# A delta rule on 32-row tiles and a soft mixture of experts: experts on the four column groups of TensorE, routing with phi as the stationary operand

## The chip, the cores and the metric

One core of a Trainium2 chip runs the whole program. The metric is the device time of one execution in microseconds (us); lower is better. Of three executions of the kernel before the median is 769.14 us (764.82 to 784.38). TensorE is called PE, VectorE DVE, ScalarE ACT, GpSimd POOL and SyncE SP, as the profile has them; SP issues most of the DMAs.

## The reference

```python
k_n = k / (norm(k) + 1e-6)                     # B=4, H=8, S=768, D=48
for t in range(S):                             # the delta rule
    y[t]  = q[t] @ state
    state = state + beta[t] * outer(k_n[t], v[t] - k_n[t] @ state)
x = y.transpose(0, 2, 1, 3).reshape(3072, 384)
logits = x @ phi                               # phi 384x32: 8 experts, 4 slots each
d = exp(logits - logits.max(0)); d /= d.sum(0) + 1e-9
slot_input = d.T @ x                           # 32x384
for e in range(8):                             # w1[e] 384x1024, w2[e] 1024x384
    slot_out[4e:4e+4] = relu(slot_input[4e:4e+4] @ w1[e]) @ w2[e]
c = softmax(logits, axis=1)
out = c @ slot_out                             # 3072x384
```

## The kernel before

Everything is float32. The sequence is cut into 24 chunks of 32 positions, four chunks to a group, so there are six groups (n = 0 to 5). A tile of 128 partitions holds 4 heads times 32 positions; the other two factors of 32 (batch, two head halves) lie in the free dimension. For each group the keys are normed (`norm`), transposed and multiplied into small 32x32 blocks (`prep`); the blocks go through DRAM (`ld`, then `lb`), a triangular inverse is worked out on DVE in 31 steps of two instructions (`invert`, tiles `pr` and `tt`, L248 and L251), and comes back through DRAM (`td`) as `TT`. `chunk` then runs the recurrence: `psR`/`psY` (state times keys and queries, L288), `psW` (L299), `psS` (new state, L309), `psY` (L326), with copies on DVE and ACT between them.

When a group is done its rows `Y` are routed (`route`): `logits(b)` transposes them (L346) and multiplies by `phi` (L352, the transposed rows stationary, 32 columns moving), `over_slots` and `maximum` make the two softmaxes with a running maximum, `sums` the running denominators, `repeat` copies `d` to four partition groups by a matmul with `sel` (L410), and `slots(c)` adds d.T @ x into `sacc`: POOL spreads `dr` with the mask `hm` to 128 columns (`db`, L420), and four matmuls with `Y` stationary follow (L425). The routing of group n-1 is handed out, merged with the inverse of group n+1, in chunks 2 and 3 of group n; a scheduler then orders every engine's instructions. Each engine works through its own list in order.

After the sixth group its routing is drained alone, the pools of the attention close, and a pool `wp2` opens on their memory. `first(e)` makes each expert's hidden row transposed (L524: w1 stationary, 4 slots moving, 32 matmuls an expert), `second(e)` multiplies by w2 (L535, 384 columns moving, all 32 slots stationary with zeros for the other experts). At the end `cT` (transposed c) times `so` gives 24 output tiles (L556), copied by ACT and DVE in turn (L561, L559) and stored. A float32 matmul shows as two instructions in the trace, a transpose as one. `load_w1` fills 96 partitions by two DMAs of 48 partitions each, `load_w2` 128 partitions; both go through SP's list. Two experts' w1 are loaded ahead, at the first chunk; the other 14 matrices (each 1536 KB) are loaded from `wp2`.

Of the kernel before, what the change touches and what calls it, by code (L numbers as in the profile page):

```python
# [16 lines left out]
def kernel(  # L17
# [21 lines left out]
    nc = tc.nc  # L39
# [13 lines left out]
    NFC = F // P  # L53
    assert G == 2 and B == 4 and GC * U == C and Dm == H * D and NSL == C
# [4 lines left out]
    ps = ctx.enter_context(tc.tile_pool(name="ps", bufs=1, space=PSUM))  # L59
    dp = ctx.enter_context(tc.tile_pool(name="dp", bufs=2, space=bass.MemoryType.DRAM))  # L60
    att = ExitStack()
    io = att.enter_context(tc.tile_pool(name="io", bufs=2))
# [65 lines left out]
    sel = cpool.tile([P, GC, 4, C], F32, name="sel")  # L128
    for h in range(4):
        nc.gpsimd.tensor_copy(sel[:, :, h, :], ident.rearrange("p (c t) -> p c t", t=C))  # L130
    ones = cpool.tile([P, 1], F32, name="ones")
    nc.vector.memset(ones, 1.0)
# [12 lines left out]

    def load_w1(e, pool, bufs):
        w1t[e] = pool.tile([GD, 4, F], F32, name="w1t", tag="w1t", bufs=bufs)
        for g in range(G):
            nc.sync.dma_start(
                out=w1t[e][g * D:(g + 1) * D],  # L150
                in_=moe_w1[e, g * 4 * D:(g + 1) * 4 * D].rearrange("(h d) f -> d h f", h=4))
# [126 lines left out]
    def chunk(cc, Yn, fill):  # L278
# [49 lines left out]
        nc.scalar.activation(Yn[:, c].rearrange("p b e -> p (b e)"),  # L328
                             py.rearrange("p b g d -> p (b g d)"), ACT.Copy)
# [3 lines left out]
    dsum = cpool.tile([P, NSL], F32, name="dsum")  # L333
    sacc = cpool.tile([GD, 4, NSL], F32, name="sacc")
    mrun = cpool.tile([NSL, 1], F32, name="mrun")
    mB = {}

    def route(n, Yn):
# [4 lines left out]
        def logits(b):  # L343
            py = pt([GD, GC, P])
            for c in range(GC):
                nc.tensor.transpose(py[:, c, :], Yn[:, c, b, :], ident)  # L346
            yT = wk.tile([GD, 4, GC, C], F32, name="yT", tag="yT")
            nc.scalar.activation(yT.rearrange("p h c t -> p c h t"),  # L348
                                 py.rearrange("p c (h t) -> p c h t", h=4), ACT.Copy)
            pl = pt([P, NSL])  # L350
            for h in range(4):
                nc.tensor.matmul(pl, lhsT=yT[:, h].rearrange("p c t -> p (c t)"),  # L352
                                 rhs=phi[:, h, :], start=(h == 0), stop=(h == 3))
            nc.vector.tensor_copy(lg[:, b, :], pl)
# [14 lines left out]
        def maximum():  # L369

            cm = small.tile([P, NSL], F32, name="cm", tag="cm")
            nc.vector.tensor_reduce(cm, lg.rearrange("p b s -> p s b"), axis=AX.X, op=ALU.max)
            pm = pt([NSL, P])
            nc.tensor.transpose(pm, cm, ident)
            if n == 0:
                nc.vector.tensor_reduce(mrun, pm, axis=AX.X, op=ALU.max)
            else:
                m1 = small.tile([NSL, 1], F32, name="m1", tag="m1")
                nc.vector.tensor_reduce(m1, pm, axis=AX.X, op=ALU.max)
                nc.vector.tensor_tensor(mrun, mrun, m1, op=ALU.max)  # L380
            pmb = pt([P, NSL])
            nc.tensor.matmul(pmb, lhsT=mrun.broadcast_to([NSL, P]), rhs=ident[0:NSL, 0:NSL],
                             start=True, stop=True)
            mB[n] = small.tile([P, NSL], F32, name="mB", tag="mB")
            nc.vector.tensor_copy(mB[n], pmb)
            nc.vector.tensor_tensor(d, lg, mB[n].unsqueeze(1).broadcast_to([P, B, NSL]),
                                    op=ALU.subtract)
            nc.scalar.activation(d, d, ACT.Exp)

        def sums():  # L390
            if n == 0:
                nc.vector.tensor_reduce(dsum, d.rearrange("p b s -> p s b"), axis=AX.X,
                                        op=ALU.add)
# [12 lines left out]
        def repeat():

            pd = pt([P, GC, B, NSL])
            for c in range(GC):
                nc.tensor.matmul(pd[:, c].rearrange("p b s -> p (b s)"),  # L410
                                 lhsT=sel[:, c].rearrange("p h t -> p (h t)"),
                                 rhs=d.rearrange("p b s -> p (b s)"), start=True, stop=True,
                                 skip_group_check=True)
# [3 lines left out]
        def slots(c):  # L417
            db = wk.tile([P, B, 4, NSL], F32, name="db", tag="db")
            for b in range(B):
                nc.gpsimd.tensor_tensor(  # L420
                    db[:, b], st["dr"][:, c, b].unsqueeze(1).broadcast_to([P, 4, NSL]),
                    hm.unsqueeze(2).broadcast_to([P, 4, NSL]), op=ALU.mult)
            pa = pt([GD, 4, NSL])
            for b in range(B):
                nc.tensor.matmul(pa.rearrange("p h s -> p (h s)"), lhsT=Yn[:, c, b, :],  # L425
                                 rhs=db[:, b].rearrange("p h s -> p (h s)"),
                                 start=(b == 0), stop=(b == B - 1))
            if n == 0 and c == 0:
                nc.vector.tensor_copy(sacc, pa)
            else:  # L430
                nc.vector.tensor_tensor(sacc, sacc, pa, op=ALU.add)

        return ([lambda b=b: logits(b) for b in range(B)] + [over_slots, maximum, sums, repeat]
# [32 lines left out]
    for e in range(NW1):  # L466
        load_w1(e, wpool, NW1)
    routing = []
    for n in range(NG):
        Yn = wk.tile([P, GC, B, GD], F32, name="Y", tag="Y")  # L470
# [29 lines left out]
    wp2 = ctx.enter_context(tc.tile_pool(name="wts2", bufs=1))  # L500
    for e in range(E):
        if e >= NW1:
            load_w1(e, wp2, 4)
        load_w2(e, wp2, 5)
    pd = pt([NSL, 1])
    nc.tensor.matmul(pd, lhsT=dsum, rhs=ones, start=True, stop=True)
    rd = cpool.tile([NSL, 1], F32, name="rd")
    nc.vector.tensor_scalar(rd, pd, 1e-9, None, op0=ALU.add)
    nc.vector.reciprocal(rd, rd)

    hx = wp2.tile([P, E, NFC, NSL], F32, name="hx")
    nc.gpsimd.memset(hx, 0.0)
    pso = ps.tile([NSL, Dm], F32, name="pso", tag="psRW")

    def first(e):

        sl = slice(e * SPE, (e + 1) * SPE)
        st = {}

        def product(t):  # L520
# [70 lines left out]
```

## Time and profile before

| | us |
|---|---|
| median of three executions | 769.14 |
| lowest and highest | 764.82, 784.38 |
| profiled execution: time | 777.74 |
| its span, first to last instruction | 776.0 |
| PE matmul busy in it | 507.6 |
| DVE, ACT, POOL busy | 255.6, 112.6, 109.6 |
| mean granted clock of TensorE | 0.655 of 2.4 GHz |

The profile is of one execution, 8.6 us above the median. Its span is divided in three: up to 566 us the six groups, 566 to 597 us the last routing, 597 to 776 us experts and output. The busy share of PE is high in the last part and middling in the first, where DVE, PE, POOL and DMA follow one another.

### The profile page before, as it was taken

What the parts mean: (1) busy time and instruction counts of PE and PEld (TensorE: products, weight loads), DVE (VectorE), ACT (ScalarE), POOL (GpSimd) and SP (SyncE); (2) the same over time, 40 slices, a digit from 0 to 9 for tenths busy, and PEclk for the clock granted to TensorE, in tenths of its full rate; (3) what the DMA queues carried; (4) which work ended last, traced back from release to release, by engine and by line L of the source; (5) the groups of instructions that cost most, each with busy time, mean ns of one, the idle gap of its engine ahead of it and who ended that gap; (6) DMA issues with size and microseconds to landing.
All of it is one profiled execution on the core that took longest, in us unless ns stands there. A gap on an engine that the chain in (4) does not pass through costs nothing.

```text
span 776.0 us, 20231 instructions
## 1 busy us (share of the span) xinstructions
PE 507.6 (65%) x9068; PEld 393.3 (51%) x9068; DVE 255.6 (33%) x694; ACT 112.6 (15%) x222; POOL 109.6 (14%) x158
## 2 busy tenths in 40 slices
PE   0603617128880488508892298863868999999998
PEld 0502516116770377406671177652757957767643
DVE  2139302781228522492237712563211000000012
ACT  0301201003220133102221022210212000000011
POOL 4121100220050300502041200422004000000000
PEclk9955557556665576755965557855767576666665
DMA  6250395404520135103540022001103999910023
GB/s 115 41 116 7 67 173 85 86 6 89 109 38 1 46 66 109 19 0 67 86 85 2 32 37 62 3 1 41 17 2 126 241 251 243 230 48 1 1 100 144
DMA packets 147639, 58.10 MB, mean 75 GB/s; under 512 B 131680, under 2 KB 142944, under 8 KB 147552
## 3 DMA queue, kind: packets, MB, share of 16 engines
q1 hardware_dynamic: 141888, 55.87, 33.1%
q10 hardware_dynamic: 5664, 0.94, 0.7%
q8 instruction: 71, 1.16, 0.6%
q14 instruction: 16, 0.13, 0.1%
HBM read 45.76 MB, written 11.01 MB: 73 GB/s over the span
## 4 chain that ended last, share of the span: by engine, by line
PE 59%; DVE 19%; DMA 7%; ACT 4%; POOL 4%; issue 3%; SPq 2%; ACTq 0%
PE ph L524 11%; PE pso L535 7%; DVE tt L251 7%; DVE pr L248 7%; PE pt L199 5%; PE pt L352 5%; PE pt L425 4%; PE psW L299 4%; PE psR L288 4%; PE pout L556 4%; PE pt L214 3%; PE psY L326 3%; DMA TT<-td 2%; PE psS L309 2%; PE pt L346 2%
## 5 line engine op out<-in xcount | busy, mean ns | idle before, releaser
L199 PE MATMUL pt<-ident,Ks 128*128 128x128 f32 x96 | 39.9, 418 | 172.1 <-POOL Ks L183 137.7
L199 PEld LDWEIGHTS pt<-ident,Ks 128*128 128x128 f32 x96 | 19.9, 207 | 177.4 <-POOL Ks L183 163.3
L524 PEld LDWEIGHTS ph<-sacc,w1t 96*128 96x128 f32 x512 | 88.2, 274 | 4.2 <-issue 3.8
L524 PE MATMUL ph<-sacc,w1t 96*128 96x4 f32 x512 | 88.8, 312 | 0.2 <-ACT cT L545 0.2
L248 DVE TENSOR_TENSOR pr<-tt,lb 128x31 f32<-128x31 f32 (+15 forms) x186 | 75.9, 408 | 20.1 <-POOL lb L236 15.0
L251 DVE TENSOR_TENSOR tt<-tt,pr 128x31 f32<-128x31 f32 (+15 forms) x186 | 68.3, 367 | 5.3
L299 PE MATMUL psW<-R,TT 32*32 32x48 f32 x1536 | 37.2, 233 | 35.4 <-DMA TT<-td 32.9
L535 PE MATMUL pso<-w2t,hx 128*32 128x384 f32 x128 | 56.9, 613 | 1.7 <-DVE hx L528 1.7
L299 PEld LDWEIGHTS psW<-R,TT 32*32 32x32 f32 x1536 | 28.4, 127 | 45.7 <-issue 23.5
L528 DVE TENSOR_SCALAR hx<-ph 128x32 f32<-128x32 f32 x8 | 1.5, 192 | 141.1 <-PE ph L524 141.1
L214 PE MATMUL pt<-KQ 48*32 48x64 f32 x1536 | 41.0, 284 | 6.9 <-issue 5.0
L352 PE MATMUL pt<-phi,yT 96*128 96x32 f32 x192 | 36.9, 346 | 8.7 <-ACT yT L348 8.6
L425 PE MATMUL pt<-db,Y 128*96 128x128 f32 x192 | 35.4, 356 | 8.3 <-POOL db L420 8.3
L352 PEld LDWEIGHTS pt<-phi,yT 96*128 96x128 f32 x192 | 34.1, 266 | 13.1 <-ACT yT L348 12.0
L202 ACT ACTIVATE KQ<-pt 128x512 f32<-128x512 f32 x48 | 28.5, 597 | 76.9 <-PE pt L199 76.9
L288 PE MATMUL psR<-S,KQ 128*32 128x96 f32 x768 | 34.2, 313 | 7.7 <-DVE S L319 6.0
L302 DVE COPY U<-psW 128x384 f32<-128x384 f32 x24 | 13.4, 558 | 77.6 <-PE psW L299 77.6
L199 PE MATMUL pt<-ident,Qs 128*128 128x128 f32 x96 | 38.3, 403 | 0.0
L214 PEld LDWEIGHTS pt<-KQ 48*32 48x32 f32 x1536 | 28.4, 138 | 18.8 <-ACT KQ L202 10.1
L420 POOL TENSOR_TENSOR db<-dr,hm 128x128 f32<-128x128 f32 x96 | 35.7, 411 | 13.6 <-ACT dr L415 13.6
L425 PEld LDWEIGHTS pt<-db,Y 128*96 128x96 f32 x192 | 31.8, 223 | 11.5 <-POOL db L420 10.2
L321 ACT ACTIVATE S<-psS 48x768 f32<-48x768 f32 x23 | 18.5, 804 | 127.7 <-PE psS L309 127.7
(103 smaller groups left out, 577.3 us busy)
## 6 DMA issues: line engine op xcount, KB each, us to landing
w1t<-in_moe_w_dram SPq DMA_DIRECT2D x16, 768.0 KB
w2t<-in_moe_w_dram SPq DMA_DIRECT2D x8, 1536.0 KB
Ks<-in_k_dram SPq DMA_DIRECT2D x96, 48.0 KB
V<-in_v_dram SPq DMA_DIRECT2D x96, 48.0 KB
out_dram<-ob SPq DMA_DIRECT2D x24, 192.0 KB
Qs<-in_q_dram SPq DMA_DIRECT2D x80, 48.0 KB
ld<-Lc SPq DMA_DIRECT2D x24, 128.0 KB
lb<-ld SPq DMA_DIRECT2D x6, 512.0 KB
```

The source lines that it names most:

```text
L199: nc.tensor.transpose(tp[:, i, a, :], src[:, c, b * G:(b + 1) * G, :].rearrange("p g d -> p (g d)"), ident)
L214: nc.tensor.matmul(pg[g][rh, b], lhsT=KQ[cc][r, b, 0, rh], rhs=KQ[cc][r, b, :, rh], start=True, stop=True, skip_group_check=True)
L248: nc.vector.tensor_tensor(prv, tt[:, 0:m, j:j + 1].broadcast_to([P, m, w]), lb[:, j, j + 1:C].unsqueeze(1).broadcast_to([P, m, w]), op=ALU ...
L251: nc.vector.tensor_tensor(tt[:, 0:m, j + 1:C], tt[:, 0:m, j + 1:C], prv, op=ALU.subtract)
L288: nc.tensor.matmul(dst[hs[h], b].rearrange("p g d -> p (g d)"), lhsT=kq[:, b, a, hs[h]], rhs=old[:, h, b, :], start=(b == 0), stop=False, ...
L299: nc.tensor.matmul(pw[hs[h], u], lhsT=T[hs[h], u], rhs=R[hs[h], u], start=(u == 0), stop=True, skip_group_check=True)
L352: nc.tensor.matmul(pl, lhsT=yT[:, h].rearrange("p c t -> p (c t)"), rhs=phi[:, h, :], start=(h == 0), stop=(h == 3))
L420: nc.gpsimd.tensor_tensor(db[:, b], st["dr"][:, c, b].unsqueeze(1).broadcast_to([P, 4, NSL]), hm.unsqueeze(2).broadcast_to([P, 4, NSL]), o ...
L425: nc.tensor.matmul(pa.rearrange("p h s -> p (h s)"), lhsT=Yn[:, c, b, :], rhs=db[:, b].rearrange("p h s -> p (h s)"), start=(b == 0), stop ...
L524: nc.tensor.matmul(st["ph"][:, t, :], lhsT=w1t[e][:, h, t * P:(t + 1) * P], rhs=sacc[:, h, sl], start=(h == 0), stop=(h == 3))
L535: nc.tensor.matmul(pso, lhsT=hx[:, e, t, :], rhs=w2t[e][:, t, :], start=(e == 0 and t == 0), stop=(e == E - 1 and t == NFC - 1))
L556: nc.tensor.matmul(po, lhsT=cT[:, n, b, :], rhs=so, start=True, stop=True)
```

## The change

The routing, the expert stage and the output are written with stationary operands of 32 columns or 32 rows, so that four matmuls stand on four different 32-column groups (or 32-row groups) of the array. The delta rule itself (`norm`, `prep`, `invert`, `chunk`) stays, save that `Y` gets four more columns of ones behind its 96 and is one of two fixed tiles.

- Routing: `turn(b)` only transposes; one `logits` for the whole group multiplies with `phi` stationary (32 columns), one batch to each column group, and transposes the result back. `maximum` keeps its running maximum repeated on four partition groups and works out one factor `al` per slot. `sums` is gone: the column of ones makes the denominator in `sacc`. `repeat` takes 32 columns of the identity instead of `sel`; `slots` has 16 matmuls a chunk with 32 rows, 32 columns and 97 moving, on the four diagonal tiles, and nothing on POOL.
- Experts: four experts at a time, each on its own column group; the slots are stationary and w1 moves (512 columns), `hr` is masked, transposed by 8 transposes, and w2 moves (384 columns). At the end one matmul with `sel4` adds the four groups.
- Output: the four batches' `cT` lie on four row groups, the tiles go through six PSUM banks and six `ob` buffers instead of four and four.
- Weights: w1 and w2 lie with 12 KB in one piece per partition on 128 partitions. `wp2` and the new PSUM pool `pp` wait tile by tile for the memory they take over (`reuse_waits="tile"`), and the loads are issued in another order.

```diff
+        w1t[e] = pool.tile([P, NKT, F], F32, name="w1t", tag="w1t", bufs=bufs)
+        nc.sync.dma_start(out=w1t[e], in_=moe_w1[e].rearrange("(p k) f -> p k f", k=NKT))
-        nc.sync.dma_start(out=w2t[e], in_=moe_w2[e].rearrange("(t p) d -> p t d", p=P))
+        nc.sync.dma_start(out=w2t[e], in_=moe_w2[e].rearrange("(p t) d -> p t d", t=NFC))
...
+        def logits():
+            pl = pt([P, P])
+            for h in range(4):
+                for b in range(B):
+                    nc.tensor.matmul(pl[C * b:C * b + C], lhsT=phi[:, h, :],
+                                     rhs=st["yT"][:, b, h].rearrange("p c t -> p (c t)"),
+                                     start=(h == 0), stop=(h == 3), skip_group_check=True)
+            lT = wk.tile([P, P], F32, name="lT", tag="lT", bufs=1)
+            nc.scalar.activation(lT, pl, ACT.Copy)
+            pq = pt([P, P])
+            nc.tensor.transpose(pq, lT, ident)
+            nc.vector.tensor_copy(lg.rearrange("p b s -> p (b s)"), pq)
...
+                nc.vector.tensor_tensor(m1, mrun, m1, op=ALU.max)
+                nc.vector.tensor_tensor(al, mrun, m1, op=ALU.subtract)
+                nc.scalar.activation(al, al, ACT.Exp)
+                nc.vector.tensor_copy(mrun, m1)
...
         def slots(c):
-            db = wk.tile([P, B, 4, NSL], F32, name="db", tag="db")
+            pa = pt([P, GD + 1])
             for b in range(B):
-                nc.gpsimd.tensor_tensor(
-                    db[:, b], st["dr"][:, c, b].unsqueeze(1).broadcast_to([P, 4, NSL]),
-                    hm.unsqueeze(2).broadcast_to([P, 4, NSL]), op=ALU.mult)
...
+                for h in range(4):
+                    r = slice(C * h, C * h + C)
+                    nc.tensor.matmul(pa[r], lhsT=st["dr"][r, c, b, :], rhs=Yn[r, c, b, 0:GD + 1],
+                                     start=(b == 0), stop=(b == B - 1), skip_group_check=True)
...
+    wp2 = ctx.enter_context(tc.tile_pool(name="wts2", bufs=1, reuse_waits="tile"))
+    for e in range(E):
+        if e >= NW1:
+            load_w1(e, wp2, 4)
+        if e % 4 == 3:
+            for i in range(e - 3, e + 1):
+                load_w2(i, wp2, 6)
...
+    def first(q):
...
+        def product(f):
+            ph = bank("ph", [P, HF])
+            for k in range(NKT):
+                for j in range(4):
+                    nc.tensor.matmul(ph[C * j:C * j + C], lhsT=sl[:, k, :],
+                                     rhs=w1t[4 * q + j][:, k, f * HF:(f + 1) * HF],
+                                     start=(k == 0), stop=(k == NKT - 1), skip_group_check=True)
...
+    def second(q):
+        for t in range(NFC):
+            for j in range(4):
+                nc.tensor.matmul(pso[C * j:C * j + C], lhsT=hT[q][:, t, C * j:C * j + C],
+                                 rhs=w2t[4 * q + j][:, t, :],
+                                 start=(q == 0 and t == 0), stop=(q == 1 and t == NFC - 1),
+                                 skip_group_check=True)
...
+    first(0)
+    second(0)
+    first(1)
+    second(1)
...
+            po = bank(("ph", "tr", "po")[i % 3], [P, Dm])
+            nc.tensor.matmul(po, lhsT=cT[C * b:C * b + C, n, :], rhs=so[C * b:C * b + C],
+                             start=True, stop=True)
+            ob = wp2.tile([P, Dm], F32, name="ob", tag="ob", bufs=6)
```

PE's list in group 3, from the last product with `phi` to the slots, before (`x4` is four matmuls of one kind in a row; the size is that of the output):

```order
L352 MATMUL pt<-phi,yT 128x32 x4
L326 MATMUL psY<-U,AT 32x48 x8
L288 MATMUL psR<-S_182,KQ 32x96 x9
L374 MATMUL pt<-ident,cm 32x128
L288 MATMUL psR<-S_182,KQ 32x96 x7
L288 MATMUL psY<-S_182,KQ 32x96 x13
L382 MATMUL pt<-ident,mrun 128x32
L288 MATMUL psY<-S_182,KQ 32x96 x3
L410 MATMUL pt<-d,sel 128x128 x4
L425 MATMUL pt<-db,Y 96x128 x15
L299 MATMUL psW<-R,TT_178 32x48
```

The same place after (L349 are the logits, L355 the transpose back, L402 the repeat, L414 the slots):

```order
L340 MATMUL pt<-ident,Y_581 96x128 x4
L320 MATMUL psY<-U,AT 32x48 x32
L349 MATMUL pt<-yT,phi 32x128 x16
L282 MATMUL psR<-S_175,KQ 32x96 x5
L355 MATMUL pt<-ident,lT 128x128
L282 MATMUL psR<-S_175,KQ 32x96 x11
L282 MATMUL psY<-S_175,KQ 32x96 x16
L379 MATMUL pt<-ident,cm 128x128
L391 MATMUL pt<-ident,mrun 128x32
L402 MATMUL pt<-d,ident 32x128 x16
L414 MATMUL pt<-Y_581,dr 32x97 x34
```

The four products of L352, spread among the chunk's matmuls, became one run of 16 behind the transposes; the order from there to the slots stays.

POOL's list in group 3, before (`lb` is the scaling that the inverse starts from, L236):

```order
L366 TENSOR_TENSOR Call<-el,mx 128x128
L420 TENSOR_TENSOR db<-dr,hm 128x128 x16
L236 TENSOR_TENSOR lb<-lb,bb 128x1024
L169 TENSOR_TENSOR sq<-Ks_80 128x1536
L183 TENSOR_TENSOR Ks_80<-Ks_80,rn 128x32x48
```

The same place after:

```order
L368 TENSOR_TENSOR Call<-el,mx 128x128
L230 TENSOR_TENSOR lb<-lb,bb 128x1024
L163 TENSOR_TENSOR sq<-Ks_80 128x1536
L177 TENSOR_TENSOR Ks_80<-Ks_80,rn 128x32x48
L249 TENSOR_TENSOR tt<-tt,bb 128x1024
```

The spreading of `dr` is gone, and `lb` stands right behind `Call`; so it does in group 4.

SP's list at the end of the groups, before, with what each row waits for:

```order
L268 DMA TT_178<-td 32x8x32 [waits DMAHW1_49,PE_49]
L155 DMA w2t<-in_moe_w_dram 128x8x384 [waits DMAHW3_49,DMAHW2_49,DMAHW4_49,DMAHW1_49,DMAHW5_49,DMAHW0_49,DMAHW6_49,DVE_49,DMAHW7_49,PE_49,Activation_49]
L155 DMA w2t<-in_moe_w_dram 128x8x384
L149 DMA w1t<-in_moe_w_dram 48x4x1024 x2
L155 DMA w2t<-in_moe_w_dram 128x8x384
```

After (L145 loads w1, L149 loads w2):

```order
L262 DMA TT_171<-td 32x8x32 [waits DMAHW7_49,PE_49]
L145 DMA w1t<-in_moe_w_dram 128x3072 [waits DMAHW0_49]
L145 DMA w1t<-in_moe_w_dram 128x3072 [waits DMAHW3_49,DMAHW4_49,DMAHW2_49,DMAHW5_49,DMAHW1_49,DMAHW6_49,DVE_49,DMAHW7_49,PE_49,Activation_49]
L149 DMA w2t<-in_moe_w_dram 128x3072 [waits Activation_49]
...
L145 DMA w1t<-in_moe_w_dram 128x3072 [waits DMAHW0_49,PE_49]
L145 DMA w1t<-in_moe_w_dram 128x3072 [waits DMAHW1_49,PE_49]
L149 DMA w2t<-in_moe_w_dram 128x3072 [waits DMAHW2_49]
```

The first load no longer waits for an engine. In the program as built the PE wait of the second load is for `psW` of the last chunk, and the PE waits below the gap (w1 of experts 6 and 7, the ninth and tenth load) are for the products of `first(0)` that read their buffers last.

## Rows read from the trace of the kernel before

**Rows 1.** Busy time by stage: us, busy us (count) by engine, clock, DMA share, GB/s

```profile
97.00:116.00 19.00, 3.00 (x67) 2.77 (x67) 1.37 (x4) 0.48 (x1) 0.00 (x0) 0.59 1.01 177
116.00:566.00 450.00, 274.49 (x7367) 226.27 (x7369) 201.09 (x547) 83.36 (x158) 78.98 (x109) 0.65 0.24 47
...
597.00:744.00 147.00, 145.09 (x642) 104.81 (x640) 1.54 (x8) 0.79 (x2) 0.00 (x0) 0.67 0.61 146
```

**Rows 2.** The chain that ended last, in order of time: start, us, what

```profile
347.66 2.82 POOL Ks L183
...
437.95 2.82 POOL Ks L183
...
491.17 5.41 POOL db L420 x15
496.58 1.87 POOL lb L236
...
532.61 2.35 POOL tt L255
...
744.96 27.65 PE pout L556 x48
```

**Rows 3.** PE, POOL and DVE in group 3 in order of time: start, us, instruction

```profile
379.12 0.84 PE L288 MATMUL psY<-S,KQ 128*32 128x96 f32 x32
...
389.06 1.09 PE L346 MATMUL pt<-ident,Y 128*96 128x128 f32 x4
...
391.19 1.92 PE L352 MATMUL pt<-phi,yT 96*128 96x32 f32 x8
...
400.53 5.47 PE L425 MATMUL pt<-db,Y 128*96 128x128 f32 x30 [1.23 <-POOL db L420]
...
400.07 5.77 POOL L420 TENSOR_TENSOR db<-dr,hm 128x128 f32<-128x128 f32 x16 [0.85 <-ACT dr L415]
...
413.12 0.55 DVE L293 TENSOR_TENSOR R<-V,psR 128x384 f32<-128x384 f32 x1 [2.33 <-PE psR L288]
```

**Rows 4.** PE in order of time: matmuls on four column groups (L288) and diagonal tiles (L299)

```profile
378.44 0.87 PE L288 MATMUL psR<-S,KQ 128*32 128x96 f32 x32
...
546.41 1.51 PE L288 MATMUL psR<-S,KQ 128*32 128x96 f32 x32
...
549.12 1.50 PE L299 MATMUL psW<-R,TT 32*32 32x48 f32 x64
...
562.91 0.88 PE L299 MATMUL psW<-R,TT 32*32 32x48 f32 x64
```

**Rows 5.** Busy time by short stretches, columns as in rows 1

```profile
378.00:380.00 2.00, 1.92 (x90) 1.69 (x91) 1.04 (x3) 0.45 (x2) 0.00 (x0) 1.00 0.46 73
546.00:551.00 5.00, 4.60 (x129) 3.92 (x129) 0.78 (x2) 0.00 (x0) 0.00 (x0) 0.55 0.01 3
...
596.00:600.00 4.00, 3.72 (x32) 3.25 (x32) 0.00 (x0) 1.57 (x4) 0.00 (x0) 1.00 1.05 388
...
680.00:684.00 4.00, 3.71 (x12) 2.23 (x13) 0.19 (x1) 0.00 (x0) 0.00 (x0) 0.50 0.52 119
...
748.00:752.00 4.00, 4.00 (x9) 2.05 (x8) 0.95 (x2) 0.98 (x2) 0.00 (x0) 0.56 0.68 245
```

**Rows 6.** Groups by line and shape: count, busy us, mean ns, idle before

```profile
L535 PE MATMUL pso<-w2t,hx 128*32 128x384 f32 x128 | 56.9, 613 | 1.7 <-DVE hx L528 1.7
```

**Rows 7.** PE in the last routing in order of time

```profile
566.84 0.32 PE L346 MATMUL pt<-ident,Y 128*96 128x128 f32 x1 [0.60 <-ACT Y L328]
...
578.39 1.92 PE L352 MATMUL pt<-phi,yT 96*128 96x32 f32 x8 [0.74 <-ACT yT L348]
...
587.17 5.83 PE L425 MATMUL pt<-db,Y 128*96 128x128 f32 x32 [1.23 <-POOL db L420]
```

**Rows 8.** SP's waits (us, times, longest) and SP in order of time

```profile
SPq L155 <- PE pt L425: 28.6, 1, 28.6
...
593.07 1.03 SPq L155 DMA_DIRECT2D w2t<-in_moe_w_dram  x2
```

More of the change, by code (lines that the diff above doesn't have):

```diff
@@ L53 @@
     NFC = F // P
+    NKT = Dm // P
     assert G == 2 and B == 4 and GC * U == C and Dm == H * D and NSL == C
@@ L127 @@
     nc.vector.tensor_reduce(tri, bdm.rearrange("p h t -> p t h"), axis=AX.X, op=ALU.add)
[L128 to L132, printed above, removed]
     TTs = [wk.tile([P, U, C], F32, name=f"TT{i}", bufs=1) for i in range(2)]
@@ L467 @@
         load_w1(e, wpool, NW1)
+    Ys = [wk.tile([P, GC, B, GD + 4], F32, name=f"Y{i}", bufs=1) for i in range(2)]
+    for t in Ys:
+        nc.gpsimd.memset(t[:, :, :, GD:GD + 4], 1.0)
     routing = []
     for n in range(NG):
-        Yn = wk.tile([P, GC, B, GD], F32, name="Y", tag="Y")
+        Yn = Ys[n % 2]
         more = n + 1 < NG
@@ L503 @@
             load_w1(e, wp2, 4)
[L504 to L508, printed above, removed]
-    nc.vector.reciprocal(rd, rd)
[L511 to L520, printed above, removed]
-            if t == 0:
-                st["ph"] = ps.tile([P, NFC, SPE], F32, name="ph", tag="pt", bufs=2)
-            for h in range(4):
-                nc.tensor.matmul(st["ph"][:, t, :], lhsT=w1t[e][:, h, t * P:(t + 1) * P],
-                                 rhs=sacc[:, h, sl], start=(h == 0), stop=(h == 3))
-        def relu():
-            nc.vector.tensor_scalar(hx[:, e, :, sl], st["ph"], 0.0, None, op0=ALU.max)
-        return [lambda t=t: product(t) for t in range(NFC)] + [relu]
@@ L532, in second, with bank @@
-    def second(e):
-        def product(t):
-            nc.tensor.matmul(pso, lhsT=hx[:, e, t, :], rhs=w2t[e][:, t, :],
-                             start=(e == 0 and t == 0), stop=(e == E - 1 and t == NFC - 1))
-        return [lambda t=t: product(t) for t in range(NFC)]
-    cT = wp2.tile([NSL, NG, B, P], F32, name="cT")
+        if e % 4 == 3:
+            for i in range(e - 3, e + 1):
+                load_w2(i, wp2, 6)
+    def bank(tag, shape):
+        return pp.tile(shape, F32, name=tag, tag=tag, bufs=2)
@@ new lines @@
+    sel4 = wp2.tile([P, 4, C], F32, name="sel4")
+    nc.vector.tensor_reduce(sel4[:, 0, :], ident.rearrange("p (c t) -> p t c", t=C), axis=AX.X,
+                            op=ALU.add)
+    nc.vector.tensor_copy(sel4[:, 1:4, :], sel4[:, 0, :].unsqueeze(1).broadcast_to([P, 3, C]))
+    rd = cpool.tile([P, 1], F32, name="rd")
+    nc.vector.tensor_scalar(rd, sacc[:, GD:GD + 1], 1e-9, None, op0=ALU.add)
+    nc.vector.reciprocal(rd, rd)
+    pT = bank("tr", [NSL, 4, G, D])
+    for h in range(4):
+        nc.tensor.matmul(pT[:, h].rearrange("p g d -> p (g d)"), lhsT=ident[:, C * h:C * h + C],
+                         rhs=sacc[:, 0:GD], start=True, stop=True, skip_group_check=True)
@@ L541 @@
+    def second(q):
[4 more added lines that the diff above has]
+                                 start=(q == 0 and t == 0), stop=(q == 1 and t == NFC - 1),
+                                 skip_group_check=True)
+    cT = wp2.tile([P, NG, P], F32, name="cT")
     for n in range(NG):
-        pc = pt([NSL, B, P])
-        for b in range(B):
-            nc.tensor.transpose(pc[:, b, :], Call[:, n, b, :], ident)
+        pc = bank("tr", [P, P])
+        nc.tensor.transpose(pc, Call[:, n].rearrange("p b s -> p (b s)"), ident)
@@ L545 @@
         nc.scalar.activation(cT[:, n], pc, ACT.Copy)
-    for e in range(E + 1):
-        drain(merge(*([second(e - 1)] if e else []), *([first(e)] if e < E else [])))
-    so = cpool.tile([NSL, Dm], F32, name="so")
-    nc.vector.tensor_scalar(so, pso, rd, None, op0=ALU.mult)
-    pp2 = ctx.enter_context(tc.tile_pool(name="pp2", bufs=1, space=PSUM))
+    first(0)
+    second(0)
+    first(1)
+    second(1)
+    sj = wp2.tile([P, Dm], F32, name="sj")
+    nc.vector.tensor_copy(sj, pso)
+    ps4 = bank("ph", [P, Dm])
@@ L552 @@
+    nc.tensor.matmul(ps4, lhsT=sel4.rearrange("p b t -> p (b t)"), rhs=sj, start=True, stop=True)
+    so = wp2.tile([P, Dm], F32, name="so")
+    nc.vector.tensor_scalar(so, ps4, rd, None, op0=ALU.mult)
     for n in range(NG):
```

123 lines of the change are left out of this document (63 added, 60 removed).

## The prediction

> **What bounds the kernel now.** I read the busy time by stage first [rows 1]. From 597 to 744 us PE is busy 145 of 147 us and nothing else is but the DMAs, at 61% of their time. Before 566 us PE is busy 61% of the time and DVE 45%, and no engine fills the stage: there the chain of waits tells more [rows 2]. Its last piece is PE's output product, 27.65 us, so the last 179 us are PE's. In it a group is a cycle of some 89 to 90 us (the scaling of the keys on POOL at 347.66 and again at 437.95). One stretch lies outside the cycle: from 97 to 116 us PE is busy 3 of 19 us [rows 1]. Third, the lists of PE, POOL and DVE in group 3 in order of time [rows 3]: PE runs the chunk's matmuls mixed with the routing from 380 us, the last product with `phi` ends at 393.1, the slots begin at 400.5 behind the first `db`, and the inverse stands on DVE behind `R` of the next group's first chunk (L293, 413.1 to 413.7). From there to 437.9, when POOL scales the keys, DVE works through the inverse and PE has nothing. So PE's time in the routing of groups 1 to 3 counts in full, and DVE's inverse is a term that the change doesn't touch. In group 4 the inverse begins later, at 498.5, behind POOL's `lb`, which stands behind 15 `db` [rows 2].
>
> **What the tiles are worth.** All prices of the new matmuls come from two of the old ones that already stand on four column groups or four diagonal tiles [rows 4]. `psR` is 16 matmuls of 96 columns on four column groups (x32 instructions): 0.87 us in a stretch with the clock granted at 2.4 GHz and 1.51 in one that lies almost all at 1.2 (mean 0.55 of full, [rows 5]). `psW` is 32 matmuls of 48 columns on four diagonal 32x32 tiles: 0.88 and 1.50 us. Both make 0.57 ns a column at the faster level, while the second expert product, one matmul at a time, takes 56.9 us for 64 matmuls of 384 columns, 2.3 ns a column [rows 6]. So four tiles side by side cost about what one costs, and I scale by columns.
>
> [...]
>
> **The change part by part**, against the span of 776.0 us.
>
> *a. w1 loaded ahead (97 to 116 us).* The `TT` load waits behind two experts' w1, 3.15 MB, which came at 177 GB/s with the DMA engines fully busy [rows 1], so for 17 us. These go to 48 partitions each. The w2 loads, to 128 partitions, came at 388 GB/s at the start of the expert stage [rows 5]. After, w1 goes to 128 partitions as well: 3.15 MB at 388 is 8.1 us. PE and SP both wait there, so what follows moves along: -8 us, bounds 0 and -9.5.
>
> *b. Routing in groups 1 to 3.* PE's list stays in order, so I add up what stands between the end of `psY` (380.0) and the first inverse step. To the end of the logits: 16 transposes (1.09 us for four at the slower clock, [rows 3], so 0.6 to 1.09), `psW` 0.9 to 1.5, `psS` and `psY` about the same each, and the logits, 16 matmuls of 128 columns, 1.2 to 2.0 by `psR`. Sum 6.4 to 10.9, taken 7.5 since the stretch starts at the faster level: 387.5 instead of 393.1. From there to the slots 7.4 us now; added are a copy on ACT and a transpose, a copy of `cm` and three tiny DVE instructions, some 1.4 us by like ones, and 0.4 for the repeat (1.2 to 2.0 for the 1.16 it is now). Slots begin at 396.7. They are 64 matmuls of 97 columns, 4.04 times `psW`: 3.6 to 6.1 us, taken 4.8, for the 5.9 us now, which POOL's 16 `db` pace (5.77 us, [rows 3]). Together -5 us a group, bounds -1 and -8; three groups -15. The inverse starts earlier by the same. `lb`, which followed the `db`, now follows `Call` and is out of the way; what could be late next is the load it scales, for which POOL doesn't wait now.
>
> *c. Group 4.* With the `db` gone, `lb` is no longer last; the DVE list then starts the inverse behind the second of four slot sums. By b, a cycle of 90 us later, the slots begin at 487 and their half is done at 489.5: -9. The stretch to the last inverse step, 34.1 us with the routing of group 4 inside against 24.2 in group 3, holds DVE's waits for PE's routing; part of these go: -3. Sum -12, bounds -5 and -15.
>
> *d. The last routing.* Now 566.8 to some 597 [rows 7]: four times transpose, copy, product, to 580.3, slots 587.2 to 593.0, then `cT`. After: the transposes follow each other, paced by PE at about 1.1 us, to 571; logits 2.0; the same 6.9 us and 1.4 more; slots 3.6 to 6.1, taken 5.5, to 587. Then `sacc` is turned (4 matmuls, 3 transposes, two copies, 3 us) and three `cT` go ahead in PE's list, 1 us. The experts start at 591.
>
> *e. Experts.* PE has 48 matmuls of 512 and 64 of 384 columns. By `psR` each half of either takes 7.0 to 12.1 us, 28 to 48 in all, for 145 now. So the loads decide: 14 matrices of 1.573 MB, 4.05 us each at 388 GB/s. Now the first of them waits 28.6 us for the last slots [rows 8] and goes out at 593.1. After, one goes out behind the last `TT` and the next seven when `psW` of the last chunk is done, at 563.8 in today's time [rows 4]; all eight are in by 594. Expert 6's w1 then needs a buffer that `first(0)` (591 to 600, at 9 us) gives back: six loads from 600, 24.3 us, and 2 us to land: 626.5. PE meanwhile does 8 transposes (4 us), `second(0)` (9), `first(1)` (9) and 8 more transposes (4), which ends at 626 also. `second(1)` needs the last matrix: 9 us, 635.5; copy, `sel4` product, scaling: 638. Now 744.9. If PE stays at 1.2 GHz throughout it is 650, at 2.4 and 388 GB/s 634.
>
> [...]
>
> *f. Output.* Stores carry 4.72 MB. In the one window where they weren't starved they moved 245 GB/s at 68% of the DMA engines [rows 5], so 360 at full: 13.1 us, with 1 us to the first copy and 2.5 for the last to land 17 us. PE's row groups would have to overlap for that, as in `psW`; if they don't it stays at 31 (27.65 us of PE, [rows 2]). Taken 17, nearest to `psW`, which also has 32 rows: 655.
>
> Sum: -8 -15 -12 -121 = -156. Span 620, and with the 1.7 us around it 622 for the profiled execution of 777.7. That one lies 8.6 us over the median; by the ratio 0.799 the median of 769.1 becomes 614; rounded with an eye to the bounds of b and e, which have more room below, 612.
>
> **Rivals.** (1) *The loads come no faster than now.* All 22 MB took from 593 to some 682 [rows 5, 8], 247 GB/s, 6.4 us a matrix. If 128 partitions aren't what made w2 fast (the window of 388 is the stage's first full one), the eighth is in at 611 and the last at 650: +24, 636. For it: w2's later windows mix with w1 and tell nothing. Against: w1 alone made 177 at 97 us, which with 388 for w2 gives the mean.
>
> (2) *The shorter routing is swallowed before the inverse,* by DVE's list or a lower clock: b and c give nothing, 639. Against: the chain goes through PE's slots in every group.
>
> (3) *Row tiles take turns in one bank.* One at a time a matmul of 128 columns takes 0.36 us (16 in 5.83, [rows 7]); 64 of 97 columns would take 17.7 us, 13 more in each of four groups and in the last routing: 612 + 65 = 677.
>
> (4) *The loads don't start early,* because one wait in the long list of the second load is the routing's after all: loads from 587, the eighth in at 615, +15: 627. That would be the change not doing what its pool says.
>
> (5) *Slower: neither row nor column groups overlap.* The logits, repeat and slots cost 5.8, 5.8 and 17.7 us, 17 us a group more than now and 22 more in the last routing than forecast; the expert products take 0.89 us each by columns, 114 us, so they end at 716 and the output at 747: 747 + 22 + 66 - 8 = 827, some 820 by the ratio. It beats the old time from the point where four tiles side by side take as long as about three in turn; `psR` and `psW` say one.
>
> **How the numbers follow.** The forecast, 0.72 (own range 590 to 632: e between 634 and 650, b and c by their bounds, f up to 14 us worse); (1) 0.11, (2) 0.06, (4) 0.05, (3) 0.02, (5) 0.02; 0.02 lies with mishaps that leave it within 2%, about what a measurement of this kernel can tell from no change. The range takes in (1), (2) and (4) and on the low side loads and clock at their best: 588 to 646. Faster 0.96, same 0.02, slower 0.02.
>
> **What would show it.** Right: w1 at over 350 GB/s near 97 us and the `TT` wait halved; groups of about 84 us; slots of 4 to 6 us with no POOL in them; loads busy from 30 us before the experts; the two expert products at some 7 to 12 us a half, with a wait for the last w2; output near 17 us. Wrong: loads below 300 GB/s, expert matmuls at over 1 ns a column, groups still at 89 us, output matmuls one after another.

## The result and the profile after

The changed kernel takes 610.31 us (median of four, 607.18 to 612.48); the kernel before took 776.26 (median of four in the same comparison, 764.82 to 784.38). The ratio is 0.794, 95% interval 0.788 to 0.800; it is taken over fast executions alone, and two of the four before (784.38 and 783.39) were slow, so it lies above the quotient of the two medians, 0.786. The profiled execution took 610.76 us with a span of 609.0; the span before was 776.0.

Busy time near the first wait, of the kernel after: stretch, us, busy us (count) of PE, its weight loads, DVE, ACT and POOL, granted clock, DMA share, GB/s.

```profile
100.00:104.00 4.00, 2.24 (x64) 2.00 (x64) 1.28 (x4) 0.40 (x1) 0.00 (x0) 0.80 0.92 336
104.00:108.00 4.00, 0.00 (x0) 0.00 (x0) 0.00 (x0) 0.00 (x0) 0.00 (x0) 0.63 0.98 403
```

The two w1 that came at 177 GB/s [rows 1] now come at about 400. The chain of the same execution (start, us, what) shows the `TT` load behind them and then the groups:

```profile
89.04 2.80 DMA td<-tt
...
100.27 10.51 DMA TT<-td
110.92 1.92 PE psW L293 x64
...
161.59 2.75 POOL Ks L177
...
210.02 2.87 PE pt L414 x128
...
244.18 2.79 POOL Ks L177
...
328.37 2.79 POOL Ks L177
...
377.98 3.13 PE pt L414 x72
381.17 1.46 PE pt L414 x52
...
412.78 2.79 POOL Ks L177
...
481.43 5.44 PE pt L414 x128
...
491.42 2.35 POOL tt L249
```

The same places in the chain of the kernel before, as far as the rows above lack them:

```profile
86.14 2.82 DMA td<-tt
...
115.86 2.02 PE psW L299 x64
...
166.36 2.75 POOL Ks L183
...
222.29 5.83 PE pt L425 x32
...
258.62 2.82 POOL Ks L183
...
597.37 23.54 PE ph L524 x128
```

L177 is the scaling of the keys, L414 the slots. Where the scalings stood 90.3 us apart (347.66 and 437.95, [rows 2]) they now stand 84.4 apart, and the `tt` of group 4 comes 78.6 us after the last of them (before 94.7). No `db` of POOL is left in the chain, and group 3's slots, at 378.0, take some 4.6 us. The last routing in the chain:

```profile
527.10 0.33 PE pt L340
...
528.10 1.82 PE pt L340 x8
...
530.59 1.60 PE pt L349 x26
...
539.57 5.44 PE pt L414 x128
...
548.38 0.98 PE ph L553 x2
```

From the first transpose (527.10) to the first expert product it is 21.3 us; before it was from 566.84 [rows 7] to 597.37, 30.5 us. Then the expert stage, first by stretches (columns as above), then by line (busy us, mean ns of one, idle before), then in the chain:

```profile
528.00:552.00 24.00, 18.48 (x239) 12.47 (x243) 5.08 (x24) 4.96 (x15) 0.83 (x4) 0.72 1.01 424
552.00:556.00 4.00, 4.00 (x34) 1.20 (x26) 0.00 (x0) 0.69 (x1) 0.00 (x0) 1.00 0.18 74
...
560.00:580.00 20.00, 13.89 (x114) 4.59 (x106) 1.44 (x2) 1.27 (x2) 0.00 (x0) 0.99 1.00 423
580.00:584.00 4.00, 1.75 (x12) 0.60 (x16) 0.00 (x0) 0.00 (x0) 0.00 (x0) 0.50 0.07 28
...
596.00:600.00 4.00, 4.00 (x15) 3.24 (x16) 2.06 (x4) 1.89 (x4) 0.00 (x0) 0.57 1.03 366
```

```profile
L553 PE MATMUL ph<-w1t,sl 128*32 128x512 f32 x96 | 14.7, 597 | 1.8 <-DMA w1t<-in_moe_w_dram 1.8
L577 PE MATMUL pso<-w2t,hT 128*32 128x384 f32 x128 | 14.4, 558 | 5.9 <-DMA w2t<-in_moe_w_dram 5.4 <-ACT hT L567 0.6
```

```profile
564.45 17.76 DMA w2t<-in_moe_w_dram
582.25 7.36 PE pso L577 x58
...
591.87 0.58 PE ph L603
```

The loads run at 424 GB/s from 20 us ahead of the first product. One of the eight went out at 512; at the next SP's list stood 11.2 us, so from 520 to 524 the DMAs moved 6 GB/s. The reader is to see two things more: the hole at 552 to 556, where SP's list stands at the first w1 that needs a buffer back, and that the last w2, not PE, starts the last half of the second product. After that load 58 of the half's 64 instructions take 7.36 us, where all 64 of the first half took 5.4: the granted clock was 0.50 at 580 to 584, at whose start PE still waited for that load. Mean ns are not costs here: 597 ns an instruction times 96 would be 57 us, the busy time is 14.7, so four run at once. The output begins at 591.9 and ends with the span at 609.0, 17.1 us.

### The profile page after: what moved, and what is told of

It reads as the page before. It is cut to its first block, busy times and chain, and to the rows that moved or that the text cites. A ratio compares the mean times of both kernels' runs of the same rounds, so it can differ in the third digit from the quotient of the medians.

```text
span 609.0 us, 20685 instructions
## 1 busy us (share of the span) xinstructions
PE 333.6 (55%) x9387; PEld 252.6 (41%) x9387; DVE 253.1 (42%) x661; ACT 113.5 (19%) x232; POOL 71.2 (12%) x62
## 4 chain that ended last, share of the span: by engine, by line
PE 44%; DVE 26%; DMA 12%; issue 5%; ACT 5%; SPq 4%; POOL 3%; ACTq 0%; DVEq 0%
DVE pr L242 9%; DVE tt L245 9%; PE pt L193 7%; PE psW L293 5%; PE pt L208 4%; PE pt L414 4%; PE psR L282 4%; PE psY L320 3%; PE psS L303 3%; DMA w2t<-in_moe_w_dram 3%; PE psY L282 3%; PE pt L340 3%; PE pso L577 2%; DMA TT<-td 2%; DMA Qs<-in_q_dram 2%
## 5 line engine op out<-in xcount | busy, mean ns | idle before, releaser
L313 DVE COPY S<-psS 48x768 f32<-48x768 f32 x23 | 22.1, 960 | 46.0 <-ACT S L315 46.0
L282 PE MATMUL psR<-S,KQ 128*32 128x96 f32 x768 | 31.8, 303 | 8.5 <-DVE S L313 6.0
L213 DVE TENSOR_TENSOR AT<-pt,tri 128x128 f32<-128x128 f32 x48 | 12.0, 286 | 58.6 <-ACT Lc L212 58.6
L320 PE MATMUL psY<-U,AT 32*32 32x48 f32 x1536 | 29.4, 233 | 4.9 <-issue 4.1
L177 POOL TENSOR_TENSOR Ks<-Ks,rn 128x1536 f32<-128x1536 f32 x6 | 16.6, 2770 | 123.7 <-DVE pr L242 88.8
L282 PE MATMUL psY<-S,KQ 128*32 128x96 f32 x768 | 29.9, 297 | 1.7 <-issue 1.7
L282 PEld LDWEIGHTS psR<-S,KQ 128*32 128x32 f32 x768 | 23.4, 135 | 14.4 <-DVE S L313 7.9
L303 PE MATMUL psS<-U,Ks 32*48 32x48 f32 x1472 | 22.7, 242 | 11.3 <-DVE U L296 8.7
L414 PE MATMUL pt<-Y,dr 32*32 32x97 f32 x768 | 26.1, 308 | 4.0 <-ACT dr L407 4.0
L320 PEld LDWEIGHTS psY<-U,AT 32*32 32x32 f32 x1536 | 24.7, 128 | 8.1 <-issue 5.9
```

Source lines behind the costliest of these rows:

```text
L282: nc.tensor.matmul(dst[hs[h], b].rearrange("p g d -> p (g d)"), lhsT=kq[:, b, a, hs[h]], rhs=old[:, h, b, :], start=(b == 0), stop=False, ...
L303: nc.tensor.matmul(psS[DP * g:DP * g + D, h, b * D:(b + 1) * D], lhsT=K[hs[h], c, b * G + g, 0:D], rhs=Ut[hs[h], b * G + g], start=(cc == ...
L313: nc.vector.tensor_copy(dst, src)
L414: nc.tensor.matmul(pa[r], lhsT=st["dr"][r, c, b, :], rhs=Yn[r, c, b, 0:GD + 1], start=(b == 0), stop=(b == B - 1), skip_group_check=True)
```

## The experiments

Times are medians; "ratio" is against the kernel before in the same comparison (0.794 for the changed kernel). In these comparisons the kernel before took 774.05 to 778.65 us (medians), against 776.26 above, so times of two of them can be set side by side to some 0.5%. Where a difference is small it is given between the profiled spans too. Each kernel is the changed one with the edit shown, unless it says otherwise.

**One expert after the other.**

```diff
-            for k in range(NKT):
-                for j in range(4):
+            for j in range(4):
+                for k in range(NKT):
```

The same in `second`, with `t` for `k`.

> The changed kernel with the loops of both expert products turned: all matmuls of one expert (one column group) stand in a row, then those of the next. Same matmuls, same loads. Theory (the products are fast because four column groups run side by side): one at a time a 384-column matmul takes up to the 0.89 us of the kernel before, so the products, 29 us busy in the changed kernel, take 60 to 115 us; time 645 to 690 us. Rival (the gain in the experts comes from the loads alone, PE waits for them anyway): 610 to 620 us.

630.42 us (two executions), ratio 0.813. Groups by line, and the stretch of the expert stage:

```profile
L577 PE MATMUL pso<-w2t,hT 128*32 128x384 f32 x128 | 34.1, 488 | 0.6 <-ACT hT L567 0.6
L553 PE MATMUL ph<-w1t,sl 128*32 128x512 f32 x95 | 24.5, 595 | 0.0
```

```profile
548.00:606.00 58.00, 55.56 (x230) 19.54 (x225) 2.89 (x4) 2.55 (x4) 0.00 (x0) 1.00 0.42 176
```

The direction is the theory's, the size is not: 58.6 us of PE in place of 29.1, and 20 us of time (17.5 of span), not 35 to 80. Overlap halves PE's time here. The waits for loads are gone and the clock stays at 1.00, which gives part of it back. And one at a time a 384-column matmul takes 0.53 us, not the 0.89 of [rows 6]. So most of what left PE in this stage (145 us, [rows 1], to 58.6) has nothing to do with the tiles side by side, and part of it is the clock (0.67 on the mean before, 1.00 here); with the tiles go 29 more.

**Pools opened plainly.** `reuse_waits="tile"` is left out of both pools.

> The changed kernel with the pools of the expert stage opened plainly, without reuse_waits, as the kernel before had them; order of loads and everything else as in the changed kernel. Theory (the early start of the loads, at 512 us of 609, is worth time of its own): the loads of w1 of expert 2 and on go out only behind the last slots, near 546 us; 14 loads of 3.75 us then end near 600 instead of 584, time 624 to 632 us. Rival (no early start is needed, PE is late anyway): 610 to 614 us.

627.98 us, ratio 0.810. SP's waits (us in total, times, longest):

```profile
SPq L145 <- PE pt L414: 18.8, 1, 18.8
```

The load waits for the slots, and the DMAs run full from 546 to 590 us (427 GB/s). The early start is worth 14 to 18 us: 14.4 between the spans of the profiled executions, 17.7 between the medians.

**Slots in a row.**

```diff
-            for b in range(B):
-                for h in range(4):
+            for h in range(4):
+                for b in range(B):
                     r = slice(C * h, C * h + C)
```

> The changed kernel with the two loops of the slot products exchanged: the four batches of one 32-row tile stand in a row, so neighbours share their tile. Theory (the four diagonal tiles run side by side even though they write one PSUM bank): in a row they no longer overlap, 16 matmuls of a step go from some 1.3 us to 3 to 4.4, 7 to 13 us more in each of groups 1 to 4 and in the last routing; time 640 to 675 us. Rival (row tiles take turns in one bank in either order): no change, 609 to 613 us. A third outcome, 615 to 635, would say that they overlap but that other work covers part.

658.21 us, ratio 0.849. From its chain:

```profile
433.38 2.79 POOL Ks L177
...
528.13 2.35 POOL tt L249
...
578.73 11.31 PE pt L414 x128
```

The last routing's slots take 11.31 instead of 5.44 us, both at 363 ns an instruction (in the changed kernel at a granted clock of 0.50), groups 1 to 3 are 7 to 8 us longer each, and from the last scaling to `tt` it is 94.8 instead of 78.6. Together these make 44 to 45 of the 48 us. So the slots count in full in every group, and the four row tiles, which all write into `pa`, do overlap when neighbours stand on different ones: if they took turns, their order would not matter.

**w1 in pieces, twice.** First 43, 43 and 42 partitions:

```diff
-        nc.sync.dma_start(out=w1t[e], in_=moe_w1[e].rearrange("(p k) f -> p k f", k=NKT))
+        src = moe_w1[e].rearrange("(p k) f -> p k f", k=NKT)
+        for p0 in range(0, P, 43):
+            p1 = min(p0 + 43, P)
+            nc.sync.dma_start(out=w1t[e][p0:p1], in_=src[p0:p1])
```

> The changed kernel with each w1 loaded by three DMAs of 43, 43 and 42 partitions instead of one of 128; same layout, 12 KB runs. Theory of the prediction (w1 was slow because a load reached only 48 partitions): w1 falls to some 180 GB/s, the wait for the TT load near 100 us grows by 8 us, and w1 in the expert stage takes 4.5 us more each; time 625 to 640 us. Rival (it is the run length, 4 KB before and 12 KB now, or the layout in DRAM): w1 stays above 380 GB/s, time 609 to 613 us.

913.56 us, ratio 1.177, far outside of both.

```profile
110.00:120.00 10.00, 0.00 (x0) 0.00 (x0) 0.00 (x0) 0.00 (x0) 0.00 (x0) 0.50 0.06 27
```

A share of 0.06 is what one DMA engine of 16 makes, at 27 GB/s, so this answers nothing about 48 partitions. How a load is dealt to the engines no run shows. Then with `range(0, P, 48)`:

> As the kernel with w1 in three pieces, but of 48, 48 and 32 partitions, all multiples of 16, as the kernel before had 48; layout and 12 KB runs as in the changed kernel. Theory of the prediction (a load that reaches 48 partitions is slow): w1 at 170 to 240 GB/s near 100 us, the wait there 6 to 8 us longer, 3 us more for each later w1; time 620 to 635 us. Rival A (the layout of w1 before was slow for another reason, and the 43 partitions of the other run were slow because they don't divide over the 16 DMA engines): w1 stays above 380 GB/s, time 609 to 615 us. Rival B (any cut of a load into pieces is slow): over 700 us.

641.66 us, ratio 0.832.

```profile
102.00:114.00 12.00, 0.00 (x0) 0.00 (x0) 0.00 (x0) 0.00 (x0) 0.00 (x0) 0.63 0.99 196
```

All engines are busy and move 196 GB/s, where the kernel before moved 177; in the expert stage w1 runs at 194 (560 to 580 us). So 48-partition loads are slow with 12 KB runs too, and it costs 31 us (27.9 of span). By these rates a w1 takes 8.0 us instead of 3.7, an estimate of 26 us for the six of the expert stage, and the `TT` load near 100 us takes 16.6 us instead of 10.5. I had put 3 us on each of the six.

**Short runs, 128 partitions.**

```diff
-  moe_w1[e].rearrange("(p k) f -> p k f", k=NKT)
+  moe_w1[e].rearrange("(k p) f -> p k f", p=P)
```

Also w2 as `(t p)`, and the transposes' columns to match.

> The changed kernel with the rows of w1 and w2 dealt to partitions as p of (k p) and (t p): still 128 partitions and one DMA a matrix, but runs of 4 KB (w1) and 1.5 KB (w2) in DRAM instead of 12 KB; the transposes read contiguous columns in place of strided ones. Theory of the prediction (128 partitions make the loads fast): loads stay near 390 to 430 GB/s, time 608 to 614 us. Rival (the run length does): w1 falls towards 180 GB/s, w2 stays at 388 as it did in the kernel before, or falls too; time 620 to 640 us.

616.0 us, ratio 0.791: the time is 5.7 us longer and the ratio a little lower, so these runs tell no difference.

```profile
102.00:106.00 4.00, 0.00 (x0) 0.00 (x0) 0.00 (x0) 0.00 (x0) 0.00 (x0) 0.83 0.99 384
```

Loads of 4 and 1.5 KB runs come at 375 GB/s from 534 to 550 (428 in the changed kernel from 532 to 548), at 384 near 100 us. The run length costs some 5 to 12% of the rate, not half.

**Every second partition.**

```diff
+        src = moe_w1[e].rearrange("(p r k) f -> r p k f", r=2, k=NKT)
+        dst = w1t[e].rearrange("(p r) k f -> r p k f", r=2)
+        for r in range(2):
+            nc.sync.dma_start(out=dst[r], in_=src[r])
```

> The changed kernel with each w1 loaded by two DMAs of 64 partitions: the first fills partitions 0, 2, 4 and so on, the second 1, 3, 5. Same layout and 12 KB runs as in the changed kernel. Theory (what made w1 slow in the kernel before and in the run of 48, 48 and 32 is which part of the 128 partitions a load covers at a time, not how many: every second one still covers them from 0 to 127): w1 stays above 380 GB/s near 100 us, time 609 to 615 us. Rival (a load is slow because it has fewer partitions, hence fewer pieces, than 128): 64 partitions make about 177 to 260 GB/s, time 620 to 640 us. [...]

608.79 us, ratio 0.790.

```profile
104.00:108.00 4.00, 0.00 (x0) 0.00 (x0) 0.00 (x0) 0.00 (x0) 0.00 (x0) 0.61 1.01 410
```

64 partitions spread over all 128 come as fast as 128 (410 GB/s; 403 in the changed kernel at 104 to 108 us), where 48 in one piece came at 196. Which partitions a load covers decides, not how many; why, no run shows.

**Output on one row group.** `cT` is transposed batch by batch to partitions 0 to 31.

```diff
-  lhsT=cT[C * b:C * b + C, n, :], rhs=so[C * b:C * b + C],
+  lhsT=cT[:, n, b, :], rhs=so[0:C],
```

> The changed kernel with cT transposed batch by batch to partitions 0 to 31, so that all 24 output products use one row group (24 transposes of Call instead of 6). Theory (the output is 17 us because neighbours on other row groups overlap, then the stores decide): one at a time a product takes 0.6 to 1.15 us, 14 to 27.65 in all, so the output takes 17 to 31 us; with the 18 more transposes, 0.15 to 0.3 us each, time 613 to 628 us. Rival (the stores and the copies decide in either case, and before it was PE's clock): 610 to 614 us.

625.79 us, ratio 0.805. Two of the 24 output products in its chain (a row is one product), and a stretch:

```profile
594.38 0.91 PE ph L604 x2
...
608.21 1.28 PE ph L604 x2
```

```profile
598.00:622.00 24.00, 24.00 (x38) 12.39 (x38) 5.58 (x10) 4.41 (x9) 0.00 (x0) 0.50 0.44 157
```

24 products stand one after another, most of them 1.28 us at the lower level: the output takes 32.6 us, near the 31.0 of the kernel before, and stores move 157 GB/s where they moved 366. Row groups side by side are worth 15 us of the output.

**Routing alone.** The kernel before, with `route` of the changed one; its `sacc` is turned once for the old experts:

```diff
+    pf = pt([GD, P])
+    nc.tensor.transpose(pf, sacc[:, 0:GD], ident)
```

> The kernel before with the new routing alone (phi as the stationary operand, slots on diagonal 32-row tiles, no mask by POOL), w1 layout, pools, experts and output as before; sacc is turned by one transpose into the layout that the old experts read. Theory (terms b, c and d of the prediction come from the routing itself, with no help of the rest): by the trace 20 us in groups 1 to 3, 16 in group 4 and 6 to 9 in the last routing, 42 to 45 us less than the kernel before in the same call, ratio 0.94 to 0.95. Rival 2 of the prediction (the shorter routing is swallowed, the groups' gain came with the w1 loads): 0 to 10 us less, ratio 0.985 to 1.0.

737.05 us (727.31 to 740.86), ratio 0.940.

```profile
336.44 2.79 POOL Ks L180
...
419.71 2.79 POOL Ks L180
...
499.11 2.35 POOL tt L252
```

The two scalings ahead of these stand at 169.66 and 252.32: cycles of 82.7, 84.1 and 83.3 and 79.4 to `tt`, within 1.2 us of those in the changed kernel. The span is 731.7, 44.3 us shorter than before. The groups' gain is the routing's own.

**All w1 first, and more buffers.** One ring of ten for both kinds, `first(1)` ahead of `second(0)`:

```diff
-            load_w1(e, wp2, 4)
-        if e % 4 == 3:
-            for i in range(e - 3, e + 1):
-                load_w2(i, wp2, 6)
+            load_w1(e, wp2, 10)
+    for e in range(E):
+        load_w2(e, wpool if e in (4, 5) else wp2, NW1 if e in (4, 5) else 10)
```

> The changed kernel with one ring of ten buffers for both kinds of matrix: the loads are issued as w1 of experts 2 to 7, then w2 of 0 to 3, and the last four w2 take buffers that the first product of experts 0 to 3 gives back (two of them those of w1 0 and 1); PE does first(0), first(1), second(0), second(1). Theory (in the changed kernel the last loads wait for buffers, the DMAs idle 552 to 557 and PE waits 2.6 + 2.8 + 1.8 us for them): the last load ends near 573 instead of 584 and the products near 580 instead of 590; 9 to 11 us less, time 599 to 602 us. Rival (the loads decide by bytes alone, or the new order moves a wait to the last chunk): 607 to 613 us.

605.27 us, ratio 0.779: a gain of 5.0 us, half of what was expected. The last load ends at 578.6, not 573: in the last chunk SP's list stood 15.2 us behind `psY`, and the DMAs idled from 522 to 531. Then twelve buffers, with the output copied through one of them; the kernel that ran kept the twelve in one ring, not in pools of their own as its text says:

> The kernel with all of w1 first, with twelve buffers in place of ten, each in a pool of its own so that the loads go first into the places that the attention gives back first; the copies of the output use the buffer of one w1 as a ring of eight in place of six tiles, which pays for the space. Only the last two w2 (experts 6 and 7, into the two oldest w1 buffers) still wait for the first product. Theory (what is left in the expert stage is DMA time lost to buffers: the run before idled from 522 to 531 behind the last psY, and its last four loads, 557.9 to 578.6, waited for first(0)): loads without gaps end at 566 to 568, the products near 577; 7 to 9 us less than that kernel, 12 to 14 less than the changed kernel, time 596 to 600 us. Rival (the early loads slow the last chunk's TT loads, or the last load waits for the last routing in another place): 603 to 610 us.

620.74 us, ratio 0.803, worse than the rival. SP's waits say why:

```profile
SPq L145 <- PE pt L356: 22.6, 1, 22.6
SPq L145 <- PE pt L415: 9.9, 1, 9.9
```

The ring's second and third place lie where the last routing still works, and everything behind them on SP waits too. With the pools:

```diff
+    wr = [ctx.enter_context(tc.tile_pool(name=f"wr{i}", bufs=1, reuse_waits="tile"))
+          for i in range(12)]
+    wr = [wr[i] for i in [6, 7, 5, 9, 2, 0, 4, 1, 8, 3, 11, 10]]
```

> Twelve buffers as in the run before, but each in a pool of its own, dealt to the loads so that those go out first whose place the attention gives back early (in the run before all twelve were one ring, and its second and third load waited 22.6 and 9.9 us for the last routing); the last two w2 still wait for first(0), the output's copies use the buffer of w1 2 as a ring of eight. Theory (the expert stage ends when the loads end, and these end when SP's list has no wait in it): three loads by 524 us, the others without a gap to 568, products near 578, time 596 to 601 us. Rival (loads that run during the last chunk hold up its TT loads or PE by as much as they gain): 603 to 610 us.

598.4 us (596.65 to 601.63, six executions), ratio 0.771, interval 0.766 to 0.776. Stretches, and the products in its chain:

```profile
512.00:520.00 8.00, 4.65 (x205) 4.04 (x197) 2.07 (x3) 0.80 (x1) 0.00 (x0) 0.71 0.98 398
520.00:544.00 24.00, 16.93 (x363) 12.59 (x367) 3.79 (x16) 4.94 (x11) 0.40 (x1) 0.57 0.99 403
544.00:564.00 20.00, 18.13 (x207) 8.68 (x203) 3.60 (x10) 3.52 (x9) 0.00 (x0) 0.96 0.95 388
564.00:568.00 4.00, 3.04 (x32) 1.40 (x25) 1.28 (x2) 0.59 (x1) 0.00 (x0) 1.00 0.57 243
```

```profile
567.43 10.48 PE pso L580 x126
```

The loads have no hole and end before 568, and PE no longer waits for them: both halves of the second product follow each other in 10.5 us (5.4 and 7.36 in the changed kernel). This beats the changed kernel by 11.9 us.

## Why the prediction was right, step by step

The forecast, 612 us, was right, with the sum a little short: -156 us of span forecast, -167.0 measured. Between the same points of the two chains, in us (the terms add to the span's difference with three losses that were not foreseen: 2.9 up to the first `td`, 86.14 to 89.04, 1.4 between `tt` and the last routing, and 0.2 between the first `psW` and the first of the four scalings):

| term | forecast | measured | from |
|---|---|---|---|
| a, w1 ahead | -8 | -7.8 | `td` to first `psW`: 29.7 to 21.9 |
| b, three groups | -15 | -20.4 | cycles 92.3, 89.0, 90.3 to 82.6, 84.2, 84.4 |
| c, group 4 | -12 | -16.0 | last scaling to `tt`: 94.7 to 78.6 |
| d, last routing | -6 | -9.3 | first transpose to experts: 30.5 to 21.3 |
| e, experts | -101 | -104.1 | 147.6 to 43.5 |
| f, output | -14 | -13.9 | 31.0 to 17.1 |

**a** holds by its reason as well: three layouts that cover the whole of the partitions come at 384 to 410 GB/s, the one of 48 at 196. The step named 128 partitions; what counts is the cover.

**b, c and d** were undersized by some 13 us together, and group 1 (9.7, bound 8) and c (16.0, bound 15) went past their ends. Groups 2 and 3 came as priced, 4.9 and 5.9 us for 5 each, with slots of 4.6 us in group 3 for 4.8 taken. The excess of b is group 1's. There the slots took 2.87 us (from 5.83), below the bound of 3.6, at a granted clock of 1.00 from 210 to 213 us (0.63 during group 3's slots, 0.50 during the last), and the stretch from the last logits to the slots, which was to grow by 1.8 us, went from 7.9 to 6.5. The forecast calls the two levels of the clock 2.4 and 1.2 GHz; the traces give a granted share alone, 1.00 and 0.50 in its two `psR` rows (0.87 and 1.51 us), and no run shows a figure in GHz. In c the first inverse step came 10.5 us earlier behind the scaling (60.5 to 50.1 us) for 9 forecast, and from there to `tt` it is 28.6 us for 34.1, 5.6 less where 3 was taken for DVE's waits. In d the slots were right (5.44 us for 5.5); the transposes with the logits took 5.1 us for some 6.2, the stretch from there to the slots 7.4 for 8.3, and the one behind the slots 3.4 for 4. So the price of the tiles was right but for group 1, and what stood in line around them was worth more than taken. Why the stretch ahead of group 1's slots and DVE's waits gave so much was not tried.

**e** had the right chain: eight loads ahead, a wait of expert 6's w1 for `first(0)`, then six loads and half a product. From the first expert product it is 7.9 us to the end of `first(0)`, 26.0 to the start of what waited for the last w2, 7.4 for that and 2.3 to the output, where the forecast had 9, 26.5 (its own 24.3 and an estimated 2 to land make 26.3; the last `TT` load of the kernel before took 1.88), 9 and 2.5: the 3 us come from the products and hardly from the loads. Once under way the six loads ran at 423 GB/s and not 388, but from 556 to 560, where they start, it was 224. PE was busy 5.4 to 9.0 us in a half, 9 taken.

**f** was sized right, and the row groups are shown to be its cause.

**The median** was scaled to the 769.14 of three executions. The span's own ratio, 620/776, and 776.26 would have given 620. The short sum and the low base nearly cancelled, which is luck: the two us between forecast and result, and the forecast's 612/769.14 = 0.796 inside the measured 0.788 to 0.800, overstate how well the terms were known. 11 us of 167 is the better measure.

**Rivals.** (1), slow loads, falls by the rows of 424. (2) falls by the routing alone, 44 us. (3), turns in one bank, was an assumption of mine and falls by the slots in a row: an order in which they don't overlap costs 48 us (65 forecast), and the changed kernel doesn't pay it. (4) falls, with its price about right: 15 us forecast, 14 to 18 measured with plain pools. (5) was priced too high: it took 0.89 us a product from a stage where small products stood between and the clock was 0.67 on the mean [rows 1]; in turn they cost 0.51 to 0.53 us at a granted 1.00, so 58.6 us, not 114.

## What to carry to other kernels

Where a matrix is streamed past few rows, make it the moving operand first (PE's 145 us became 58.6 here, part of it by the clock); putting four such products on column groups halved what was left (58.6 to 29.1 us), and then the loads decided. When loads decide, look at the queue that issues them: the place in memory that each buffer takes over sets when the load may start, and one late place holds up all behind it (12 buffers in the wrong order 620.7 us, in the right one 598.4). A load should cover the whole range of partitions: in runs of 12 KB, 128 at once or 64 spread over all ran at over 400 GB/s here, 48 at 196 and 43 at 27.

## What the runs showed that was not expected

- A load of 43 partitions ran at 27 GB/s and a DMA share of 0.06, that of one engine of 16; one of 48 at 196 and a share of 0.99; one of every second partition, 64 in all, made 410.
- After PE had waited for the last w2, the clock was low for the work behind it: 58 instructions of the second half of the second product took 7.36 us after a wait (granted 0.50 at 580 to 584), the 64 of the first half 5.4 us. In the run with the experts in turn PE was busy 55.6 of 58 us and the clock stayed at 1.00.
- Output products on one row group stood at a granted 0.50 although PE was busy for 24 of 24 us; the expert products in turn, as busy, at 1.00. In the changed kernel the output on four row groups stood low as well, 0.57 at 596 to 600 and 0.50 at 600 to 604. Why is open; the output products use 32 rows each, the expert products 128.
